# Window attention and expert routing on one Trainium2 core: last logits in column groups, weight loads behind the gather, 128-token products first

## The chip, the cores and the metric

The kernel runs on one core of one Trainium2 chip, alone. The metric is the time of one execution on the device in microseconds (us); the median of several runs counts. The engines are TensorE (PE; its weight loads are listed apart as PEld), VectorE (DVE), ScalarE (ACT), GpSimd (POOL) and SyncE (SP). Each works through its own queue in order. Direct transfers are issued by SP and travel on the hardware queue; indirect ones (gather, scatter) and accumulating ones are issued by POOL and travel on the software queue. Both share 16 DMA engines.

## What is computed

Eight batches of 8 heads attend over 576 positions of 64 numbers, four heads in a window of 32 and four in a dilated one (every fourth of 128). The result x (4608 tokens of 512 numbers) goes through a router that gives each of 8 experts exactly 576 tokens, greedily by the largest logit, and then through that expert's two layers.

```python
attn = softmax(mask(q @ k.T / 8)) @ v
x = attn.transpose(0, 2, 1, 3).reshape(4608, 512)
logits = x @ w_gate
for idx in np.argsort(-logits.flatten()):
    tok, e = idx // 8, idx % 8
    if assigned[tok] < 0 and counts[e] < 576:
        assigned[tok] = e; counts[e] += 1
for e in range(8):
    mask = assigned == e
    out[mask] = np.maximum(x[mask] @ w1[e], 0) @ w2[e]
```

## The kernel before

Three stages follow one another. In **attention** each batch has units (kind of window, part), and each unit makes scores (L503, L506), exponentials on ACT (L456), products with v (L514, into px), a reciprocal and scaling on DVE (L520, L526, into xs) and transposes of xs on TensorE (L564), which ACT or DVE copies to xt (L272, L575). Both forms are needed: xs goes to DRAM as `xd`, and xt is what the logits are made from. Most batches make logits with the gate weights `wgp` (32 columns, 8 of them used) as the stationary operand and 288 tokens moving, the four groups g of 128 features side by side in four column groups of TensorE (L597), copied by DVE (L605) and transposed (L618). The last batch, b=7, goes through `tokens()` (L650) instead: xt is stationary there, 128 tokens at a time, 8 columns of wgp move (L664), and four operations, one for each g, have five products each: four with 128 tokens and one with 64. The results go to `Lt` (L674 and an ACT copy at L272). `R.choose` then takes each token's largest logit (M, L879), and `coarse` counts (L770).

The **router** searches the threshold at which the first expert is full, on DVE and TensorE in turn, then makes its token list `idx` (L1068 to L1102).

The **experts** take eight rounds. In a round r, SP reads the expert's number (`fetch`), POOL gathers its 576 tokens from xd in five indirect transfers (`gather`, L1249: chunks of 128, the last of 64), TensorE transposes each chunk (L1263), and ACT and DVE split it into a high and a low part, `xh` and `xl` (L1137, L1138). From round 1 on these transposes share one buffer, `ptx`. `weights(n, r, f)` loads 256 KB of w1 or w2 into a `raw` buffer (L1150), and ACT makes the high part; the low part is a DVE subtraction or, for w2 of round 0 and for w1 and w2 of round 1, an ACT copy of −high and an accumulating transfer on POOL's queue (L1158, L1160). `expert` makes GEMM1 in pieces `first(f, j)`: f is one of 8 groups of 128 hidden features, j one of two parts of the tokens, 256 or 320 wide, and a piece has 12 products (L1300: high·high, low·high, high·low for four groups of input features). GEMM2 (L1342 to L1347) adds up y, and POOL scatters it (L1368). The search for the next round (counts at L778 with ACT's copy `ohr` of the flags, a step on DVE at L815 to L828) stands among the products of the round before, and so do the gather and the transposes of every round but the first.

The order on each engine is made by a planner, `Schedule`, from operations with an engine, a cost, dependencies and a boost; what it writes out is then that engine's queue. `keep_clock` (L121) puts dummy products on TensorE where the planner sees a gap ahead of the transposes of round 0. `behind(r, f)` gives the planner a dependency of the loads of round 0 from f=3 on upon the gather's second transfer; it shapes the order, and SP's queue holds no wait for it. Round 0 has eight w1 and four w2 loads that find free buffers.

```python
RAW1, D_R, NQ, AHEAD_W = 8, 262, (2, 2), (3,)
MSZ = (128, 128, 128, 128, 64)
CUT = (0, 256, CAP)
```

Of the kernel before, what the change touches and what calls it, by code (L numbers as in the profile page):

```python
# [22 lines left out]
NE, FF = 8, 1024  # L23
# [16 lines left out]
RAW1, D_R, NQ, AHEAD_W = 8, 262, (2, 2), (3,)  # L40
# [202 lines left out]
def attention(tc, ctx, C, load_const, T, xd, Lt, R):  # L243
# [406 lines left out]
    def tokens(un):  # L650

        b, u = un.b, un.u
        c0, c1 = b * S // 128, (b * S + S) // 128
        parts = [(c, 0, 128) for c in range(-(-b * S // 128), c1)]
        half = (c0, 64, 64) if b % 2 else (c1, 0, 64)
        late = B_K if b < B - 1 else B_E
        pt = Buf(PV)
        o = lambda c, p, n: pt.tile[p:p + n, NE * (c - c0):NE * (c - c0) + NE]
# [9 lines left out]
        t = un.op("PE", 1050, lambda: logits([1]), [t], late)  # L668
        t = un.op("PE", 1050, lambda: logits([2]), [t, *ch_[b]], late)
        t = un.op("PE", 1050, lambda: logits([3]), [t, *xt_[b]], late)  # L670
        for kk in range(2):
            xt_[b, kk][2].append(t)
        ca = parts[0][0]
        xs_ = [un.op("DVE", 200, lambda: nc.vector.tensor_copy(  # L674
            Lt[:, ca:c1], pt.tile[:, NE * (ca - c0):NE * (c1 - c0)].rearrange("p (c e) -> p c e", e=NE)), [t], late),
            un.op("ACT", 250, lambda: act(Lt[half[1]:half[1] + 64, half[0]], o(*half)), [t], late)]
        pt.users += xs_
        if b < B - 1:
            hl_.append(xs_[1])
        x = un.op("DVE", 1000, lambda: R.choose(c0, c1), [*xs_, *(hl_ if b == B - 1 else ())], late)  # L680
        coarse(c0, c1, x, B_P if b < B - 1 else late - u * P_U)
# [425 lines left out]
def moe(tc, ctx, C, R, xd, w1, w2, out):  # L1107
# [31 lines left out]
    E, gemm1_end, x_users, got = {}, {}, {}, {}  # L1139

    def weights(n, r, f, deps):

        raw, old, use = RAW[n].take()

# [97 lines left out]
    def gather(r, ix, box):  # L1242

        done = []
        for m, n in enumerate(MSZ):
# [6 lines left out]
            g = op("POOL", 1040, get, [ix, *old], B_G, lat=T_G if r else 2600)  # L1252
# [26 lines left out]
    def gemm(cost, fn, deps):  # L1279
        last[0] = op("PE", cost, fn, [*deps, last[0]])  # L1280
        return last[0]

    def expert(r, X, box, W1, W2):
# [3 lines left out]
        def first(f, j):  # L1287
            ph, old, use = PHR[j].take()
            h, l, hi, lo, useh, usel = W1[f]
            c0, c1 = CUT[j:j + 2]  # L1290
            o = ph[:, :c1 - c0]
            xs = X[:2] if j == 0 else X[2:]
# [11 lines left out]
            for k in range(0, 3 * ND, n):  # L1304
# [7 lines left out]
                g = gemm(n * ((c1 - c0) / 2.4 + 13.5), lambda part=part: mm(part), deps)  # L1312
            useh.append(g)
# [14 lines left out]

        for f, j in ((0, 0), (1, 0), (0, 1), (1, 1), *((f, j) for f in range(2, NF) for j in range(2))):
            first(f, j)  # L1330
# [52 lines left out]
    def round_(r):  # L1383
# [6 lines left out]
        W[r] = [weights("1", r, f, [en, *behind(r, f)]) for f in range(NF)]  # L1390

    def behind(r, f):

        return [got[r, 1]] if r < len(AHEAD_W) and f >= AHEAD_W[r] else []

    round_(0)
    for r in range(NE):
        W2 = [weights("2", r, f, [EN[r], *behind(r, NF)]) for f in range(NF)]
        expert(r, X[r], BOX[r], W[r], W2)
        if r + 1 < NE:  # L1400
            round_(r + 1)
# [78 lines left out]
```

## Time and profile before

| what | value |
|---|---|
| runs | 713.92, 715.23, 717.02 us (median 715.23) |
| the profiled execution's own time | 717.54 us |
| its span, first to last instruction | 715.8 us |
| mean granted TensorE clock | 0.962 of full speed |
| TensorE busy | 673.1 us, 94% of the span |
| VectorE, ScalarE, GpSimd busy | 485.2, 292.0, 137.7 us |
| chain that ended last | TensorE 73%, issue 12%, VectorE 6%, DMA 4%, GpSimd 3% |

The span covers the instructions of the profiled execution; about 1.7 us of its time lie around it. Busy shares are means over stages with different limits, so the rows further down are of single places.

### The profile page before, as it was taken

The numbers are of one execution on the slowest core, as the hardware profiler recorded it, in microseconds if no ns is written. First come the engines' busy times: TensorE is split into PE (matmuls) and PEld (weight loads), VectorE is DVE, ScalarE is ACT, GpSimd is POOL, SyncE is SP. The second block draws the span as 40 slices with busy tenths as digits, with TensorE's granted clock in tenths as the row PEclk, the third lists the DMA queues.
The fourth block names the chain that finished last, engine by engine and source line by source line (L and its number), as shares of the span: only waits on it lengthen the run. The fifth ranks groups of instructions, "written<-read, shape, count | busy, mean of one in ns | idle before, by whom it ended". The sixth has DMA issues, their size and how long they took to land.

```text
span 715.8 us, 17384 instructions
## 1 busy us (share of the span) xinstructions
PE 673.1 (94%) x6577; PEld 590.1 (82%) x6579; DVE 485.2 (68%) x2085; ACT 292.0 (41%) x616; POOL 137.7 (19%) x204
## 2 busy tenths in 40 slices
PE   7899999999974799799999999999999999999995
PEld 5788899989973598689889779879978978988984
DVE  5467867778447789589679878968877964823300
ACT  3345554553520483576234423523523534424310
POOL 6111111100000332641410310310311131221011
PEclk9899999999975799999999999999999999999998
DMA  9999999982210674987323513602621384123001
GB/s 251 267 252 263 277 321 234 281 225 56 68 35 33 212 155 112 286 184 222 97 67 119 170 63 91 217 31 56 227 87 53 124 286 143 50 70 97 1 22 44
DMA packets 58524, 104.60 MB, mean 146 GB/s; under 512 B 6212, under 2 KB 27844, under 8 KB 58436
## 3 DMA queue, kind: packets, MB, share of 16 engines
q1 hardware_dynamic: 49096, 78.32, 38.5%
q0 software_dynamic: 9344, 25.17, 12.8%
q8 instruction: 51, 0.84, 0.5%
q14 instruction: 33, 0.27, 0.1%
HBM read 78.31 MB, written 18.87 MB: 136 GB/s over the span
## 4 chain that ended last, share of the span: by engine, by line
PE 73%; issue 12%; DVE 6%; DMA 4%; POOL 3%; ACT 1%; SPq 0%; POOLq 0%; DVEq 0%
PE ph L1300 24%; PE py L1342 15%; PE pS L506 9%; PE px L514 6%; PE pS L503 3%; PE px L564 3%; DMA xg<-xd,idx 2%; PE pm L486 2%; PE pz L778 2%; PE ptx L1263 2%; PE py L1345 1%; POOL out L1368 1%; PE py L1347 1%; DMA qs<-in_qd 1%; PE px L597 1%
## 5 line engine op out<-in xcount | busy, mean ns | idle before, releaser
L1342 PE MATMUL py<-w2h,hb 128*128 128x512 f32 x512 | 172.5, 401 | 1.3 <-issue 1.3
L1300 PE MATMUL ph<-xh,w1h 128*128 128x256 f32 (+1 forms) x512 | 138.7, 301 | 0.0
L1300 PE MATMUL ph<-xl,w1h 128*128 128x256 f32 (+1 forms) x512 | 136.2, 296 | 0.0
L1300 PE MATMUL ph<-xh,w1l 128*128 128x256 f32 (+1 forms) x512 | 136.0, 296 | 0.0
L1342 PEld LDWEIGHTS py<-w2h,hb 128*128 128x128 f32 x512 | 96.7, 189 | 21.5 <-issue 2.4
L1137 ACT ACTIVATE hb<-ph 128x256 fp32r<-128x256 f32 (+2 forms) x192 | 59.8, 346 | 103.9 <-PE ph L1300 103.5
L1342 PE MATMUL py<-w2l,hb 128*128 128x512 f32 x256 | 100.9, 394 | 0.7 <-DVE w2l L1138 0.5
L1300 PEld LDWEIGHTS ph<-xh,w1h 128*128 128x128 f32 x512 | 91.5, 189 | 0.6 <-ACT xh L1137 0.2
L1300 PEld LDWEIGHTS ph<-xh,w1l 128*128 128x128 f32 x512 | 91.6, 190 | 0.0
L1300 PEld LDWEIGHTS ph<-xl,w1h 128*128 128x128 f32 x512 | 91.5, 190 | 0.0
L506 PE MATMUL pS<-q,k 128*80 128x96 f32 (+1 forms) x672 | 83.7, 266 | 0.0
L1368 POOL DMA_INDIRECT out<-y,idx x40 | 40.1, 1003 | 203.6 <-ACT y L1137 142.8
L1320 DVE SCALAR_TENSOR_TENSOR hb<-ph,hb 128x320 fp32r<-128x320 f32 (+1 forms) x128 | 57.4, 453 | 29.7 <-ACT hb L1137 26.8
L456 ACT ACTIVATE E<-pS 96x384 f32<-96x384 f32 (+1 forms) x96 | 46.8, 487 | 74.9 <-PE pS L506 73.3
L506 PEld LDWEIGHTS pS<-q,k 128*80 128x80 f32 (+1 forms) x672 | 69.2, 160 | 0.3 <-issue 0.3
L1137 ACT ACTIVATE y<-py 128x512 f32<-128x512 f32 (+1 forms) x40 | 23.9, 597 | 103.4 <-PE py L1342 90.8
L493 DVE CUSTOM_DVE_ANT_0 junkm<-pm,const 128x80 bf16<-128x80 f32 (+1 forms) x336 | 59.7, 243 | 7.8 <-PE pm L486 7.5
L1342 PEld LDWEIGHTS py<-w2l,hb 128*128 128x128 f32 x256 | 48.5, 190 | 10.3 <-DVE w2l L1138 1.1
L514 PE MATMUL px<-v,E 81*64 81x65 f32 (+1 forms) x1344 | 48.3, 225 | 4.4 <-ACT E L456 2.5
L514 PEld LDWEIGHTS px<-v,E 81*64 81x64 f32 (+1 forms) x1344 | 43.1, 138 | 9.2 <-issue 2.9
L1137 ACT ACTIVATE w1h<-raw 128x512 fp32r<-128x512 f32 x64 | 38.5, 628 | 29.2 <-DMA raw<-in_moe_w 28.8
L1249 POOL DMA_INDIRECT xg<-xd,idx x40 | 40.3, 1007 | 50.1 <-PE ph L1300 31.1
(171 smaller groups left out, 1019.1 us busy)
## 6 DMA issues: line engine op xcount, KB each, us to landing
raw<-in_moe_w SPq DMA_DIRECT2D x128, 256.0 KB, 4.4
v<-in_vp SPq DMA_DIRECT2D x8, 780.0 KB
v<-in_vd SPq DMA_DIRECT2D x8, 650.0 KB
xd<-xs SPq DMA_DIRECT2D x16, 288.0 KB, 6.8
xd<-xs SPq DMA_DIRECT2D x32, 144.0 KB, 10.6
w2l<-raw POOLq DMA_DIRECT2D x16, 256.0 KB
qs<-in_qp SPq DMA_DIRECT2D x7, 576.0 KB, 9.2
k<-in_kp SPq DMA_DIRECT2D x7, 576.0 KB, 10.4
```

The source lines that it names most:

```text
L456: e = self.op("ACT", 380, lambda j=j, pS=pS: nc.scalar.activation(self.E[:self.nk, j * self.gs:j * self.gs + self.gs], pS.tile[:, :self.gs ...
L493: nc.vector.tensor_tensor_reduce(out=jk[:, c - c0, :nk], in0=pm[:, (c - c0) * nk:(c - c0 + 1) * nk], in1=mm[:, min(1, (c if self.kind == 0 ...
L503: nc.tensor.matmul(pS[:nk, c - c0], ls[:64 + n, c], self.r[:64 + n, :2 * nq], start=(c == c0), stop=False, skip_group_check=True)
L506: nc.tensor.matmul(pS[:nk, c - c0], self.Ks[c], self.Qm[c], start=False, stop=True, skip_group_check=True)
L514: nc.tensor.matmul(px[64 * a:64 * a + 64, c - c0], lh, self.V[c][a], start=True, stop=True)
L564: nc.tensor.transpose(t[:, c], src, C["identf"])
L1137: act = lambda o, i, f=AF.Copy: nc.scalar.activation(o, i, f)
L1249: nc.gpsimd.indirect_dma_start(out=xg[:n], out_offset=None, in_=xd, in_offset=bass.IndirectOffsetOnAxis(ap=box[0][:n, m:m + 1], axis=0))
L1300: nc.tensor.matmul(o, a[:, d * 128:d * 128 + 128], b[:, d, c0:c1], start=((d, i) == pairs[0]), stop=((d, i) == pairs[-1]))
L1320: hl = op("DVE", 335 if j == 0 else 400, lambda: nc.vector.scalar_tensor_tensor(hb[:, CAP + c0:CAP + c1], o, 0.0, hb[:, c0:c1], op0=OP.max ...
L1342: nc.tensor.matmul(py, x, w, start=(f + i == 0), stop=(f == NF - 1 and i == 2))
L1368: s = nc.gpsimd.indirect_dma_start(out=out, out_offset=bass.IndirectOffsetOnAxis(ap=box[0][:n, m:m + 1], axis=0), in_=y[:n], in_offset=None)
```

## The change

Three edits go together.

First, `tokens()`: wgp[:, g] is now stationary and the tokens move; the four chunks of 128 tokens stand side by side in four column groups, and the piece of 64 goes to the first. DVE then copies 128x192 to the tile `lg`, TensorE transposes it back (`gates`), and the two copies to Lt follow. The planner's cost of each of the four groups goes from 1050 to 330.

Second, the weight loads: in round 0 from f=3 on and in round 1 from f=4 on, a POOL memset of one element of the raw buffer, put behind the gather, stands between; the SP load of that buffer waits for it, and all loads behind it on SP's queue with it.

Third, in round 0 the pieces (f=0, j=0) and (f=1, j=0) are each made in two halves of 128 tokens, chunk 0 of both and then chunk 1 of both: 48 products of 128 columns where 24 of 256 stood.

```diff
-RAW1, D_R, NQ, AHEAD_W = 8, 262, (2, 2), (3,)
+RAW1, D_R, NQ, AHEAD_W = 8, 262, (2, 2), (3, 4)
...
-        def logits(gs):
-            for c, p, n in parts + [half]:
-                for g in gs:
-                    t0 = 128 * c + p - b * S
-                    nc.tensor.matmul(o(c, p, n), xt_[b, g // 2][0][:, g % 2, t0:t0 + n], wgp[:, g, :NE],
-                                     start=(c == parts[0][0] and g == 0), stop=(g == 3), skip_group_check=True)
-
-        t = un.op("PE", 1050, lambda: logits([0]), [*xt_[b][:3], ready["w"]], late, pt)
...
+        def logits(g):
+            x = xt_[b, g // 2][0][:, g % 2]
+            for k in range(c1 - c0):
+                nc.tensor.matmul(pt.tile[32 * k:32 * k + 32, :128], wgp[:, g], x[:, t0 + 128 * k:t0 + 128 * k + 128],
+                                 start=(g == 0), stop=(g == 3), skip_group_check=True)
+            nc.tensor.matmul(pt.tile[:32, 128:128 + t0], wgp[:, g], x[:, :t0], start=False, stop=(g == 3), skip_group_check=True)
+
+        t = un.op("PE", 330, lambda: logits(0), [*xt_[b][:3], ready["w"]], late, pt)
...
+        k = un.op("DVE", 330, lambda: nc.vector.tensor_copy(lg[:, :128 + t0], pt.tile[:, :128 + t0]), [t, *L4_["free"]], late)
+        pt.users.append(k)
+
+        def gates():
+            nc.tensor.transpose(pg.tile[:, :128], lg[:, :128], C["identf"])
+            nc.tensor.matmul(pg.tile[128 - t0:, 128:160], lg[:32, 128:128 + t0], C["identf"][:32, :32], start=True, stop=True)
...
         raw, old, use = RAW[n].take()
+        if n == "1" and r < len(AHEAD_W) and f == AHEAD_W[r]:
+
+            gate[r] = op("POOL", 100, lambda: nc.gpsimd.memset(raw[:1, :1], 0.0), [got[r, 1], *old], B_G)
+        if r in gate:
+            deps = [*deps, gate[r]]
...
-            g = op("POOL", 1040, get, [ix, *old], B_G, lat=T_G if r else 2600)
+            g = op("POOL", 1250, get, [ix, *old], B_G, lat=T_G if r else 2500)
...
+        if r == 0:
+
+            two = [PHR[0].take() for _ in range(2)]
+            for m in range(2):
+                ends = [products(f, 0, two[f], X[m:m + 1], 128 * m, 128 * m + 128) for f in range(2)]
+            for f in range(2):
+                hide(f, 0, two[f], ends[f])
         for f, j in ((0, 0), (1, 0), (0, 1), (1, 1), *((f, j) for f in range(2, NF) for j in range(2))):
-            first(f, j)
+            if r or f > 1 or j:
+                first(f, j)
...
-    def behind(r, f):
-
-        return [got[r, 1]] if r < len(AHEAD_W) and f >= AHEAD_W[r] else []
```

`products` and `hide` are `first` cut in two: its twelve products, and what ACT and DVE do with their sum.

How the order on the engines moves is seen at three places. The first is TensorE at the end of attention; L514 are the last products with v, L564 transposes, L664 (after: L662 and L664) the logits of b=7. Before:

```order
L506 MATMUL pS_137<-q_102,k_98 80x96 x4
L664 MATMUL px_139<-wgp,xt_126 128x8 x4
L664 MATMUL px_139<-wgp,xt_126 64x8
L514 MATMUL px_140<-v_104,E_111 64x65 x3
L514 MATMUL px_140<-v_104,E_111 64x65 [waits Activation_49]
L514 MATMUL px_140<-v_104,E_111 64x65 x8
L564 MATMUL px_138<-const_63,xs_122 128x128 [waits DVE_49]
L564 MATMUL px_138<-const_63,xs_122 128x128 x2
L564 MATMUL px_140<-const_63,xs_122 128x128 [waits DVE_49]
L564 MATMUL px_140<-const_63,xs_122 128x128 x2
L664 MATMUL px_139<-wgp,xt_126 128x8 [waits DVE_49,Activation_49]
L664 MATMUL px_139<-wgp,xt_126 128x8 x3
```

After:

```order
L514 MATMUL px_140<-v_104,E_111 64x65 x8
L564 MATMUL px_139<-const_63,xs_122 128x128 [waits DVE_49]
...
L564 MATMUL px_139<-const_63,xs_122 128x128 [waits Activation_49]
L564 MATMUL px_139<-const_63,xs_122 128x128 x2
L662 MATMUL px_138<-xt_124,wgp 32x128 [waits Activation_49]
L662 MATMUL px_138<-xt_124,wgp 32x128 x3
L664 MATMUL px_138<-xt_124,wgp 32x64
...
L662 MATMUL px_138<-xt_126,wgp 32x128 [waits DVE_49,Activation_49]
L662 MATMUL px_138<-xt_126,wgp 32x128 x3
L664 MATMUL px_138<-xt_126,wgp 32x64
L676 MATMUL px_140<-const_63,L_127 128x128 [waits DVE_49]
L677 MATMUL px_140<-const_63,L_127 64x32
```

Before, three of the four logits groups stand ahead of the last L514 (two of them above these rows); after, all four stand behind the last transposes, four sets of which now follow L514, and behind them the two products of `gates`.

The second place is TensorE at the start of round 0, where xg is the gathered chunk, `ph` the sum of GEMM1 and L778 (after: L782) a count of the search. Before:

```order
L1263 MATMUL py_3205<-const_63,xg_3252 128x128 [waits DMASW0_49]
L1263 MATMUL py_3205<-const_63,xg_3252 128x128 x3
L121 LDWEIGHTS zero
L121 MATMUL ph_3202<-zero 128x512
L1263 MATMUL py_3206<-const_63,xg_3253 128x128 [waits DMASW1_49]
...
L1263 MATMUL ptx_3207<-const_63,xg_3254 128x128 [waits DMASW2_49,DVE_49]
L1263 MATMUL ptx_3207<-const_63,xg_3254 128x128 x3
L1300 MATMUL ph_3201<-xh,w1h_3220 128x256 [waits Activation_49]
L1300 MATMUL ph_3201<-xh,w1h_3220 128x256 x3
L1300 MATMUL ph_3201<-xh,w1l_3236 128x256 x4
L1263 MATMUL py_3205<-const_63,xg_3255 128x128 [waits DMASW3_49,DVE_49]
```

After:

```order
L1272 MATMUL py_3208<-const_63,xg_3255 128x128 [waits DMASW0_49]
L1272 MATMUL py_3208<-const_63,xg_3255 128x128 x3
L782 LDWEIGHTS ohr [waits Activation_49]
L782 MATMUL pz<-G,ohr 128x4x16 [waits DVE_49]
...
L1272 MATMUL py_3209<-const_63,xg_3256 128x128 [waits DMASW1_49]
L1272 MATMUL py_3209<-const_63,xg_3256 128x128 x3
L1308 MATMUL ph_3204<-xh,w1h_3223 128x128 [waits Activation_49]
L1308 MATMUL ph_3204<-xh,w1h_3223 128x128 x3
L1308 MATMUL ph_3204<-xh,w1l_3239 128x128 x4
L1272 MATMUL ptx_3210<-const_63,xg_3257 128x128 [waits DMASW2_49]
L1272 MATMUL ptx_3210<-const_63,xg_3257 128x128 x3
L1308 MATMUL ph_3204<-xl,w1h_3223 128x128 [waits DVE_49]
```

GEMM1 (L1300, after: L1308) began behind the transposes of three chunks and now begins behind those of two; the nine counts, which stood behind 40 products of GEMM1, now stand between the two chunks' transposes, and the single dummy products between them are gone.

The third place is POOL, SP and ACT in round 1. POOL before (w1l is an accumulating transfer, out a scatter, xg the gather):

```order
L1160 DMA w1l_3236<-raw_3208 128x512 [waits DMASW6_49,DMAHW0_49,PE_49,Activation_49]
L1160 DMA w1l_3237<-raw_3209 128x512 [waits DMASW7_49,DMAHW1_49,PE_49,Activation_49]
L1160 DMA w1l_3238<-raw_3210 128x512 [waits DMASW0_49,DMAHW2_49,PE_49,Activation_49]
L1367 MEMSET spacer 1x1 [waits Pool_49]
L1368 DMA out<-y_3269,idx 4608x512 [waits DMASW1_49,Activation_49]
L1249 DMA xg_3252<-xd,idx 128x512 [waits DMASW2_49,DVE_49]
L1249 DMA xg_3253<-xd,idx 128x512 [waits DMASW3_49]
...
L1249 DMA xg_3256<-xd,idx 64x512 [waits DMASW6_49]
L1160 DMA w1l_3239<-raw_3211 128x512 [waits DMASW7_49,DMAHW3_49,PE_49,Activation_49]
L1160 DMA w1l_3240<-raw_3212 128x512 [waits DMASW0_49,DMAHW4_49,PE_49,Activation_49]
```

POOL after:

```order
L1394 MEMSET spacer 1x1 [waits Pool_49]
L1395 DMA out<-y_3272,idx 4608x512 [waits DMASW1_49,Activation_49]
L1258 DMA xg_3255<-xd,idx 128x512 [waits DMASW2_49,DVE_49]
L1258 DMA xg_3256<-xd,idx 128x512 [waits DMASW3_49]
...
L1258 DMA xg_3259<-xd,idx 64x512 [waits DMASW6_49]
L1150 MEMSET raw_3215 1x1
L1169 DMA w1l_3242<-raw_3214 128x512 [waits DMASW7_49,DMAHW3_49,PE_49,Activation_49]
L1394 MEMSET spacer 1x1 [waits Pool_49]
L1395 DMA out<-y_3273,idx 4608x512 [waits DMASW0_49,Activation_49]
L1169 DMA w1l_3243<-raw_3215 128x512 [waits DMASW1_49,PE_49,DMAHW4_49,Activation_49,Pool_49]
```

SP after, in the same round (raw_3215 is the buffer of f=4):

```order
L1159 DMA raw_3213<-in_moe_w 128x512 [waits DMAHW2_49,DVE_49]
L1159 ISA
L1159 DMA raw_3214<-in_moe_w 128x512 [waits DMAHW3_49,DVE_49]
L1159 ISA
L1159 DMA raw_3215<-in_moe_w 128x512 [waits DMAHW4_49,DVE_49,Pool_49]
L1159 ISA
L1159 DMA raw_3216<-in_moe_w 128x512 [waits DMAHW5_49,DVE_49,Activation_49]
L1159 ISA
L1159 DMA raw_3219<-in_moe_w 128x512 [waits DMAHW6_49,DMASW1_49,Activation_49]
```

ACT after, in the same round:

```order
L1141 ACTIVATE xh<-ptx_3210 128x4x128 [waits PE_49]
L1141 ACTIVATE xh<-ptx_3210 128x4x128 [waits DVE_49,PE_49]
L1141 ACTIVATE w1h_3227<-raw_3215 128x512 [waits DMAHW4_49,Pool_49]
L1141 ACTIVATE y_3271<-py_3209 128x512 [waits DMASW5_49,PE_49]
L1167 ACTIVATE w1l_3243<-w1h_3227 128x512 [waits Activation_49]
L1141 ACTIVATE w1h_3228<-raw_3216 128x512 [waits DMAHW5_49]
L1141 ACTIVATE xh<-ptx_3210 128x4x128 [waits DVE_49,PE_49]
```

POOL's memset follows the fifth gather, the load of f=4 waits for it on SP, and eight more loads stand behind that one. On ACT the split of f=4 (w1h_3227) now stands behind xh of chunks 0 and 1 and ahead of a y, and that of f=5 ahead of xh of chunk 2.

## Rows read from the trace of the kernel before

**Rows 1.** The page, part 2: TensorE in 40 slices of 17.9 us.

```profile
PE   7899999999974799799999999999999999999995
```

**Rows 2.** Chain that ended last, 195 to 212 us: start us, us, what.

```profile
195.55 1.11 PE px L597 x16
198.54 0.33 PE px L564 x3
198.87 1.00 PE px L664 x10
204.92 0.76 PE px L514 x23
206.61 0.56 PE px L564 x3
207.20 0.67 DVE xt L575
208.01 2.17 PE px L664 x10
210.63 0.21 DVE M L879
```

**Rows 3.** Windows: length, busy us (instructions) by engine, granted clock, DMA share, GB/s.

```profile
208.00:210.00 2.00, 1.99 (x10) 1.98 (x10) 0.00 (x0) 0.00 (x0) 0.00 (x0) 0.50 0.65 166
```

**Rows 4.** Timeline, round 0: start, us, engine, line, what, [idle before].

```profile
237.33 1.45 POOL L1249 DMA_INDIRECT xg<-xd,idx  x1 [3.35 <-DVE idx L1102]
240.50 0.46 DVE L889 TENSOR_TENSOR oh<-Lt,Mo 128x288 bf16<-128x288 f32 x1
242.97 0.66 PE L1263 MATMUL py<-const,xg 128*128 128x128 f32 x4 [1.75 <-DMA xg<-xd,idx]
244.97 0.74 PE L1300 MATMUL ph<-xh,w1h 128*128 128x256 f32 x4
245.53 1.16 ACT L902 ACTIVATE ohr<-oh 128x1152 bf16<-128x1152 bf16 x1
248.47 0.64 PE L1300 MATMUL ph<-xl,w1h 128*128 128x256 f32 x4
```

**Rows 5.** Windows, columns as in rows 3: round 0's gather, then round 2's.

```profile
230.00:241.50 11.50, 6.17 (x31) 2.37 (x30) 10.84 (x30) 2.27 (x4) 4.58 (x4) 0.51 0.90 307
341.75:342.25 0.50, 0.50 (x4) 0.42 (x3) 0.50 (x2) 0.50 (x1) 0.32 (x1) 1.00 0.00 0
342.25:343.50 1.25, 1.25 (x8) 1.02 (x7) 1.25 (x4) 0.04 (x1) 0.97 (x1) 1.00 0.77 210
```

**Rows 6.** Timeline of POOL: first gather of round 2.

```profile
340.54 1.08 POOL L1249 DMA_INDIRECT xg<-xd,idx  x1 [7.13 <-issue]
```

**Rows 7.** Timeline, round 1: weight loads on SP, gathers, ACT, TensorE.

```profile
279.55 32.42 SPq L1150 DMA_DIRECT2D raw<-in_moe_w  x13
289.25 1.04 POOL L1249 DMA_INDIRECT xg<-xd,idx  x1 [0.30 <-DVE A L1049]
294.38 0.92 POOL L1249 DMA_INDIRECT xg<-xd,idx  x1 [0.30 <-issue]
298.55 0.63 ACT L1137 ACTIVATE w1h<-raw 128x512 fp32r<-128x512 f32 x1 [4.68 <-DMA raw<-in_moe_w]
298.76 0.66 PE L1263 MATMUL ptx<-const,xg 128*128 128x128 f32 x4 [4.00 <-DMA xg<-xd,idx]
```

**Rows 8.** Windows, columns as in rows 3: before and behind the wait in round 1.

```profile
289.50:294.50 5.00, 5.00 (x31) 3.90 (x29) 3.20 (x11) 3.76 (x6) 3.78 (x5) 1.00 1.10 263
299.10:302.70 3.60, 3.60 (x20) 2.91 (x19) 2.17 (x9) 1.19 (x3) 3.00 (x6) 0.54 1.11 207
```

**Rows 9.** DMA, 289 to 291 us: software queue's packets, MB, share of 16 engines.

```profile
q0 software_dynamic: 133, 0.25, 67.5%
```

**Rows 10.** Timeline of weight loads of GEMM1, round 0.

```profile
255.01 0.19 PEld L1300 LDWEIGHTS ph<-xh,w1h 128*128 128x128 f32 x1
255.12 0.19 PEld L1300 LDWEIGHTS ph<-xh,w1l 128*128 128x128 f32 x1
```

More of the change, by code (lines that the diff above doesn't have):

```diff
@@ L652, in tokens @@
         b, u = un.b, un.u
[L653 to L655 removed]
+        c0, c1 = -(-b * S // 128), (b * S + S) // 128
+        t0 = 128 * c0 - b * S
         late = B_K if b < B - 1 else B_E
[L657 to L665 removed]
@@ L667, in tokens @@
[L667 to L670 removed]
+        pt, pg = Buf(PV), Buf(PV)
+        lg = L4.tiles[0][:, (b % 2) * S:]
+        def logits(g):
[4 more added lines that the diff above has]
+            nc.tensor.matmul(pt.tile[:32, 128:128 + t0], wgp[:, g], x[:, :t0], start=False, stop=(g == 3), skip_group_check=True)
@@ L671, in tokens @@
+        t = un.op("PE", 330, lambda: logits(0), [*xt_[b][:3], ready["w"]], late, pt)
+        t = un.op("PE", 330, lambda: logits(1), [t], late)
+        t = un.op("PE", 330, lambda: logits(2), [t, *ch_[b]], late)
+        t = un.op("PE", 330, lambda: logits(3), [t, *xt_[b]], late)
         for kk in range(2):
             xt_[b, kk][2].append(t)
-        ca = parts[0][0]
-        xs_ = [un.op("DVE", 200, lambda: nc.vector.tensor_copy(
-            Lt[:, ca:c1], pt.tile[:, NE * (ca - c0):NE * (c1 - c0)].rearrange("p (c e) -> p c e", e=NE)), [t], late),
-            un.op("ACT", 250, lambda: act(Lt[half[1]:half[1] + 64, half[0]], o(*half)), [t], late)]
@@ L683, in attention @@
+        t = un.op("PE", 180, gates, [k], late, pg)
+        xs_ = [un.op("DVE", 200, lambda: nc.vector.tensor_copy(
+            Lt[:, c0:c1], pg.tile[:, :128].rearrange("p (c e) -> p c e", e=32)[:, :, :NE]), [t], late),
+            un.op("ACT", 250, lambda: act(Lt[128 - t0:, c0 - 1], pg.tile[128 - t0:, 128:128 + NE]), [t], late)]
+        pg.users += xs_
+        x = un.op("DVE", 1000, lambda: R.choose(c0 - 1, c1), [*xs_, *hl_], late)
+        coarse(c0 - 1, c1, x, late - u * P_U)
     ch_, hl_ = {}, []
@@ L1285, in expert, with products @@
         hidden = {}
[L1287 to L1292, printed above, removed]
+        def products(f, j, ring, xs, c0, c1):
+            ph, old, _ = ring
+            h, l, hi, lo, _, _ = W1[f]
+            o = ph[:, c0 - CUT[j]:c1 - CUT[j]]
             pairs = [(d, i) for d in range(ND) for i in range(3)]
@@ L1327, in first @@
                 done.append(h2)
+        def first(f, j):
+            ring = PHR[j].take()
+            hide(f, j, ring, products(f, j, ring, X[:2] if j == 0 else X[2:], *CUT[j:j + 2]))
+        if r == 0:
[4 more added lines that the diff above has]
+                hide(f, 0, two[f], ends[f])
         for f, j in ((0, 0), (1, 0), (0, 1), (1, 1), *((f, j) for f in range(2, NF) for j in range(2))):
-            first(f, j)
+            if r or f > 1 or j:
+                first(f, j)
         gemm1_end[r] = last[0]
@@ L1389, in round_ @@
         X[r] = gather(r, ix, BOX[r])
-        W[r] = [weights("1", r, f, [en, *behind(r, f)]) for f in range(NF)]
-    def behind(r, f):
-        return [got[r, 1]] if r < len(AHEAD_W) and f >= AHEAD_W[r] else []
+        W[r] = [weights("1", r, f, [en]) for f in range(NF)]
     round_(0)
     for r in range(NE):
-        W2 = [weights("2", r, f, [EN[r], *behind(r, NF)]) for f in range(NF)]
+        W2 = [weights("2", r, f, [EN[r]]) for f in range(NF)]
         expert(r, X[r], BOX[r], W[r], W2)
```

13 lines of the change are left out of this document (7 added, 6 removed).

## The prediction

> **What bounds the kernel now.** I read the page's slices first. TensorE's row stands at nine nearly everywhere and falls in two places: slices 11 to 13 (197 to 250 us: the end of attention, the router's search, the start of round 0) and slice 16 (286 to 304 us: the start of round 1) [rows 1]. All three edits act there, so each place is read by itself; elsewhere the time is TensorE's own work, and a part that moves no TensorE work there changes nothing.
>
> End of attention, by the chain of work that ended last [rows 2]: up to 205.68 it is TensorE all the way, and three of its pieces are logits groups of L664 (the first is shown, 1.00; three alike make 3.0). After the last score-times-value products (204.92 + 0.76) no TensorE work covers anything: scale, transposes, the DVE copy of xt, then the fourth logits group, 2.17 long, and the router's first instruction M at 210.63. The window shows why that group took twice as long as the other three: granted clock 0.50, the lower of the two levels, 1.2 GHz [rows 3], behind the 0.83 between the transposes' end (207.17) and 208.01 in which TensorE only waited for the copy.
>
> Start of round 0, by the timeline [rows 4]: the first gather is issued at 237.33; TensorE, busy with dummy products until 241.22, then waits 1.75 for the chunk and starts transposing at 242.97. GEMM1 starts at 244.97 and its part j=0 of f=0,1 ends at about 248.95 (the last four start at 248.47). The windows show the DMA engines at a 0.90 share, 307 GB/s, up to 241.5, when twelve weight loads are under way [rows 5]. For comparison round 2's gather, issued at 340.54 on idle queues, has no data until 342.25 and carries it in the next 1.25 us [rows 5, 6]: about 3.0 us from issue to landed chunk.
>
> Start of round 1 [rows 7]: weight loads are issued from 279.55 on, the first gather at 289.25, the last of its five at 294.38, but TensorE waits 4.00 us for the first chunk, until 298.76. In 289.5 to 294.5 the DMA share is 1.10 [rows 8]; the software queue, which carries the gather and ahead of it three accumulating w1l transfers and a scatter, moves only 0.25 MB in 289 to 291, one chunk's worth [rows 9]. After the stall the granted clock is 0.54 for 3.6 us [rows 8]: of these about 1.7 are lost (3.6 × 0.46). So this place costs 5.7.
>
> **Part 1, logits (A).** Before, the three covered groups cost 3.0 on the path, and two transposes of another unit stood ahead too (0.33 each [rows 2]); by the order both now stand behind the last products. So those end at about 205.68 − 3.0 − 0.66 = 202.0. From there: normalizing as before (0.93: 205.68 to 206.61), transposes 0.56, a copy of xt 0.67, making 204.2. Then twenty logits products: L597, which puts 288 columns in the same column groups, runs 16 in 1.11 [rows 2]; the new ones have at most 128 columns. They cannot be cheaper than that by much (0.069 each), so five of the last group 0.35, up to 1.4 for all twenty if nothing is ready earlier. The added copy of 128x192 is bounded by the Lt-sized DVE instruction (M, 0.21) and the xt copy (0.67): I take 0.35. The added transposes are two of a trio that takes 0.33 to 0.56: 0.3. The copies to Lt as before: 0.45 from the end of the group at 210.18 to M. Six hand-overs at 0.03 to 0.04 give 0.2. The sum is 205.8 to 206.9 at the full clock; at half clock transposes and logits double, up to 207.6. M was at 210.63: a gain of 3.0 to 4.8. I take **A = −3.4**, on the cold side, since TensorE stands there as before. If side-by-side groups ran one after another (20 at the 0.10 that L664 pays) and cold, the gain would fall to about 1.5.
>
> **Part 2, round 0 (B).** The loads of f=3 on wait behind the POOL memset, which stands behind all five gathers, so only three of twelve compete with the gather. Chunk 0 lands at 237.33 + 3.0 to 3.3, 240.6 at the latest, before the dummies end: the wait of 1.75 goes. But the order puts the first nine counts (0.46) between the transposes of chunks 0 and 1. They need ACT's copy ohr: its source is ready at 240.96 and it takes 1.16 [rows 4], thus 242.15. Then: transposes 241.22 to 241.88, counts to 242.65, chunk 1's transposes to 243.3, GEMM1 from there (244.97 before), a gain of 1.7. Against it stand 48 products of 128 columns in place of 24 of 256. The trace has none with such weights. Those of 256 columns follow one another at about 0.12 (24, with 1.06 of transposes among them, in 244.97 to 248.95). The lower bound from columns alone would be half of that, 0.06; the upper is 0.12, no change per product. The nearest row is the weight load: at a change of operand two of 128 columns start 0.11 apart [rows 10], and the L664 products, eight columns wide with the same 128-column weights, take 0.10 each [rows 2]. That is weight load and nothing else, so I take 0.115: 48 × 0.115 = 5.5 against 24 × 0.12 = 2.9. With the transposes of chunks 2 to 4 between (0.6, 0.6, 0.46) part j=0 ends at 243.3 + 5.5 + 1.7 = 250.5; the counts in it (0.46) stood later before. **B = 250.5 − 0.46 − 248.95 = +1.1**; by 0.06 a product it would be −1.5.
>
> The rule that bears on this: the Trainium skill, "TensorE: Matmul & The Clock Gate", section "Back-to-back issue gap", gives about 81 ns for each pair of weight load and 128-column product in a stream. By it the sum would be 1.6 lower (48 × 0.034); no row here shows so short a pair with fp32r weights of 128 columns, so it is a rival below.
>
> The gated loads cost nothing here: f=3's issue at about 244 plus 3 to 4 us is 248, while f=0 to 2 cover it: 36 products of 256 columns at 0.12 and 36 of 320 at, by their columns, 0.15 are 9.7 from 243.3 on, so f=3 is due at 253 or later. With that cover gone, each us is a us.
>
> **Part 3, round 1 (C).** Ungated are only f=0 to 3, issued from 279.55: 1.05 MB, which at the 307 GB/s of [rows 5] is through by 283, well ahead of the gather; f=4 and the eight loads behind it on SP's queue stay away until about 295.6. The software queue then has its three transfers and scatter done near 290, and chunk 0, at 3.0 us from issue, lands at 292.3 to 293. TensorE comes to it at 294.76. Stall and clock drop go: −5.7. Late next is DVE: the order puts a search step ahead of xl, and the single transpose buffer then holds the next chunk up; I give 0.4 for it. **C = −5.3**, between −6 and −3.
>
> What the gate delays: behind the load of f=4 on ACT stand y of m=3 and, behind f=5, xh of chunk 2 (order above). f=4 lands at about 295.6 + 3 = 298.6, f=5 near 299.5; xh of chunk 2 ran at 306.07 before, so is due at about 300.5. A us or so of slack. GEMM1 of round 1 takes f=4 about 13 us after its start, far behind. In before ACT itself stood for f=7's load until 298.55, ahead of all xh [rows 7]; that wait now comes behind chunks 0 and 1.
>
> **The rest (D)**: in rounds 3 to 7 counts and ranks stand about one group earlier. TensorE is at nine tenths or more in each of those slices, with nothing long to win: 0, give or take 1.
>
> **Sum**: −3.4 + 1.1 − 5.3 = −7.6, from the profiled execution's own 717.54 to 709.9. That execution lies 2.3 above the median 715.23, so against the runs shown: **707.6**.
>
> **Rivals.**
> *128-column products are cheap* (0.06 to 0.08 each): B turns −0.5 to −1.5, total 705.0 to 706.0. For it: no row has a stream of them, and the 0.11 is one change of operand; against: [rows 10], and L664 beside it.
> *Column groups serial, or tail cold throughout*: A = −1.5, total 709.5. Against it is L597.
> *The round-1 gather stays late*: the accumulating transfers and the scatter on its own queue, not the loads, hold it. For it: the software queue alone reaches a share of 67.5% in 289 to 291 [rows 9]. Then 2 to 4 us of stall and part of the low clock remain, C = −1 to −3, total 710 to 712.
> *The gate itself becomes the wait* (the slower side): ACT is in order, so a gated load f=4 or f=5 that lands late holds xh of chunk 2, the single transpose buffer and TensorE. If the nine loads meet a gather still in its queue (1.2 MB at 0.13 MB/us, the rate of [rows 9], is 9 us: 304), the stall is 4 plus a low clock of 1.7, so C is near 0, total 713. It makes the kernel slower by 0.5% only if f=5 lands more than 11 us behind its due time, after about 311.5; then 719 and up.
> *Reordered later rounds open new waits*: several of 1 to 2 us, total 709 to 711.
>
> **Chances.** Main case 0.47 (705.5 to 709.5); cheap products 0.14; tail 0.09; gather late 0.14; gate 0.10, of which 0.03 slower; later rounds 0.06. The bound of 0.5% (about what a measurement of this kernel can tell from no change) is 711.65 and 718.8. Faster: all of main, cheap, tail, 0.05 of later rounds and 0.09 of gather late: 0.84; slower 0.03; the same 0.13. For 8 in 10 the range is 703.0 to 712.5: it leaves out the gate case and the best ends of all parts together.
>
> **What would show it.** Right: M some 3 to 4.5 us earlier; no wait for xg before the first transposes of either round; the granted clock at 1.0 behind round 1's gather; 128-column products spaced 0.11 or more. Wrong: spacing of 0.08 or less (B); a TensorE wait on xg near 293 (C); ACT waiting for raw with xh behind it; SP's gated loads landing after 301.

## The result, and the profile after

The changed kernel ran at 706.46, 708.50, 709.66 and 710.48 us, median 709.08, against 716.01 for four runs of the kernel before: ratio 0.9876, 95% interval 0.9827 to 0.9925. The forecast was 707.6, a change of −7.6; the measured one is −6.9. A second set of runs gave 0.9847 (0.9803 to 0.9890). So the sum held. Its terms did not: they erred on both sides and cancelled, which is luck.

The profiled execution took 706.46 us, the fastest of the four, while that of before (717.54) was slower than all four of its own, so the two spans lie 11.2 apart, more than the medians. The page after, to be read beside [rows 1]:

```profile
span 704.6 us, 17434 instructions
...
PE   7899999999964999899999999999999999999995
...
PEclk9999999999985899999999999999999999999998
```

Counted from 0, slice 13, the start of round 0, now stands at nine; slices 11 and 12 still hold the search, and slice 16 is at eight where it was at seven. Next the chain of the changed kernel at the end of attention (start us, us, what), which answers to [rows 2]:

```profile
195.60 0.87 PE px L514 x24
...
198.04 0.92 PE px L564 x6
198.96 0.40 PE px L662 x8
...
199.40 0.28 PE px L662 x6
...
200.55 0.37 DVE L L672
...
200.97 0.33 PE px L676
...
202.06 0.21 DVE M L883
```

The chain leaves the products with v at 196.47 for DVE (the last of them end at 197.15 in the timeline), not at 205.68, and M starts at 202.06, not at 210.63. The logits now are one run of 0.40, 0.28 and so on behind the transposes, about 1.5 in all, where the last group alone took 2.17, but DVE's copy and the transposes back follow: from the last products to the first gather both kernels take the same time, 31.6 and 31.7.

Behind M the stages run like this (TensorE, its weight loads and POOL in the timeline: start, us, engine, line, what, idle before and what ended it), beside [rows 4]:

```profile
228.75 1.46 POOL L1258 DMA_INDIRECT xg<-xd,idx  x1 [3.35 <-DVE idx L1106]
...
232.66 0.44 PEld L1272 LDWEIGHTS py<-const,xg 128*128 128x128 f32 x4 [0.93 <-DMA xg<-xd,idx]
232.66 0.68 PE L1272 MATMUL py<-const,xg 128*128 128x128 f32 x4
...
233.64 0.46 PE L782 MATMUL pz<-G,ohr 128*128 128x64 bf16 x9 [0.29 <-issue]
...
234.48 0.64 PE L1308 MATMUL ph<-xh,w1h 128*128 128x128 f32 x4
...
240.10 0.61 PE L1308 MATMUL ph<-xh,w1h 128*128 128x128 f32 x4
...
240.55 0.61 PE L1308 MATMUL ph<-xh,w1l 128*128 128x128 f32 x4
...
241.00 0.61 PE L1308 MATMUL ph<-xl,w1h 128*128 128x128 f32 x4
...
241.44 0.80 PE L1308 MATMUL ph<-xh,w1h 128*128 128x320 f32 x4
```

The transposes start 3.9 behind the gather's issue, where it was 5.6. TensorE shows no wait for the chunk, but only because its dummy products end at 232.64, just when the chunk is there; the first weight load had waited 0.93 for it. Fours of 128-column products start at 240.10, 240.55, 241.00 and 241.44, so one product takes 0.112. And round 1, beside [rows 7]:

```profile
281.67 1.03 POOL L1258 DMA_INDIRECT xg<-xd,idx  x1 [0.30 <-DVE A L1053]
...
286.98 0.46 PE L782 MATMUL pz<-G,ohr 128*128 128x64 bf16 x9
...
287.28 0.63 PE L1272 MATMUL ptx<-const,xg 128*128 128x128 f32 x4
...
290.47 0.32 DVE L819 STREAM_TRANSPOSE Q<-pz 128x128 f32<-128x128 f32 x1 [3.67 <-remote]
290.53 0.60 ACT L1141 ACTIVATE xh<-ptx 128x512 fp32r<-128x512 f32 x1 [4.79 <-remote]
...
292.62 0.45 PE L782 MATMUL pz<-G,ohr 128*128 128x64 bf16 x9 [2.63 <-DVE G L796]
```

The transposes of chunk 0 start at 287.28 with no wait, 5.6 after the gather's issue. But the 4.00 of before is not simply gone. The nine counts ahead of them end at 287.44, and DVE, which only needs their result (Q), starts at 290.47; ACT starts xh at 290.53, though its transposes ended at 287.91. "Remote" means that the profile found the update of the semaphore that both waited for, just ahead of their start, and no instruction that ended there. TensorE, which has recorded products up to 289.99, then stands until DVE's step is done, at 292.62, and the low clock follows (windows: length, busy us by engine, granted clock, DMA share, GB/s; compare [rows 8]):

```profile
281.70:287.20 5.50, 5.50 (x39) 4.26 (x38) 3.29 (x12) 1.76 (x2) 4.28 (x5) 1.00 0.73 214
290.00:292.60 2.60, 0.00 (x0) 0.00 (x0) 1.96 (x9) 0.60 (x1) 0.09 (x1) 1.00 0.93 232
294.20:297.60 3.40, 3.40 (x10) 2.47 (x9) 1.89 (x6) 2.00 (x4) 0.00 (x0) 0.50 0.92 351
```

So the gather meets a DMA share of 0.73 where it met 1.10, and still TensorE lost 2.6 and then half of the 3.4 that it ran at a granted clock of 0.50, which is 1.2 GHz.

From starts in the traces of all profiled executions one gets a table by stage. "v" is the end of the last products with v, "gather" the first gather's issue in round 0, G1 and G2 the first product of GEMM1 and GEMM2 in a round, "the end" the start of the last instruction. Rows in bold are the kernel before and the changed one.

| kernel | start to v | v to gather | gather to G2, round 0 | to G1, round 1 | to G1, round 2 | to the end |
|---|---|---|---|---|---|---|
| **before** | 205.66 | 31.67 | 37.02 | 36.01 | 58.43 | 346.93 |
| **before, again** | 205.22 | 31.67 | 37.12 | 35.92 | 58.45 | 345.41 |
| **changed** | 197.15 | 31.60 | 37.99 | 35.91 | 59.24 | 342.63 |
| **changed, again** | 198.20 | 31.59 | 37.90 | 32.78 | 59.40 | 343.05 |
| tokens_only | 197.16 | 31.60 | 39.97 | 37.02 | 58.44 | 344.83 |
| tokens_undone | 206.34 | 31.67 | 37.87 | 31.21 | 60.48 | 343.30 |
| no_gate | 201.72 | 31.61 | 40.17 | 35.49 | 58.93 | 342.70 |
| gate1_only | 201.49 | 31.61 | 40.14 | 31.23 | 60.50 | 342.67 |
| split_undone | 203.31 | 31.61 | 36.62 | 31.20 | 58.94 | 343.26 |
| cost_back | 196.46 | 31.60 | 38.68 | 30.54 | 60.11 | 343.11 |
| tokens_1050 | 202.98 | 31.34 | 37.86 | 31.23 | 60.53 | 342.62 |
| no_split_cost | 198.41 | 31.62 | 37.24 | 30.65 | 60.62 | 342.92 |

The kernels below the bold rows are the experiments that follow. Ratios are to runs of the kernel before on the same chip; the two kernels again, no_gate and tokens_only ran on one chip (chip 2), tokens_1050 and no_split_cost on another (3) and the other four on a third (13). Which chip the first profiles of the two kernels are from is not on record.

### The profile page after: what moved, and what is told of

It reads as the page before. It is cut to its first block, busy times and chain, and to the rows that moved or that the text cites. A ratio compares the mean times of both kernels' runs of the same rounds, so it can differ in the third digit from the quotient of the medians.

```text
span 704.6 us, 17434 instructions
## 1 busy us (share of the span) xinstructions
PE 667.7 (95%) x6602; PEld 586.8 (83%) x6604; DVE 484.9 (69%) x2086; ACT 291.8 (41%) x616; POOL 137.9 (20%) x206
## 4 chain that ended last, share of the span: by engine, by line
PE 68%; issue 12%; DVE 9%; DMA 6%; POOL 2%; ACT 1%; another core or an unknown queue 1%; POOLq 0%; SPq 0%; DVEq 0%
PE ph L1308 18%; PE py L1369 18%; PE pS L506 8%; PE px L514 5%; DMA qs<-in_qd 3%; PE px L564 3%; PE pS L503 2%; PE pm L486 2%; PE ptx L1272 2%; PE pz L782 2%; PE py L1372 1%; PE py L1374 1%; DMA v<-in_vd 1%; DVE hb L1335 1%; POOL out L1395 1%
## 5 line engine op out<-in xcount | busy, mean ns | idle before, releaser
L1308 PE MATMUL ph<-xh,w1h 128*128 128x256 f32 (+2 forms) x520 | 139.2, 299 | 0.0
L1308 PE MATMUL ph<-xl,w1h 128*128 128x256 f32 (+2 forms) x520 | 138.0, 297 | 0.0
L1308 PE MATMUL ph<-xh,w1l 128*128 128x256 f32 (+2 forms) x520 | 137.0, 295 | 0.0
L1308 PEld LDWEIGHTS ph<-xh,w1h 128*128 128x128 f32 x520 | 92.8, 190 | 0.5
L1308 PEld LDWEIGHTS ph<-xh,w1l 128*128 128x128 f32 x520 | 92.7, 190 | 0.0
L1308 PEld LDWEIGHTS ph<-xl,w1h 128*128 128x128 f32 x520 | 92.4, 190 | 0.1
L514 PE MATMUL px<-v,E 81*64 81x65 f32 (+1 forms) x1344 | 47.0, 224 | 1.8 <-ACT E L456 1.7
L514 PEld LDWEIGHTS px<-v,E 81*64 81x64 f32 (+1 forms) x1344 | 42.1, 137 | 6.4 <-ACT E L456 1.8
```

The lines of the kernel that those rows point to most:

```text
L514: nc.tensor.matmul(px[64 * a:64 * a + 64, c - c0], lh, self.V[c][a], start=True, stop=True)
L1308: nc.tensor.matmul(o, a[:, d * 128:d * 128 + 128], b[:, d, c0:c1], start=((d, i) == pairs[0]), stop=((d, i) == pairs[-1]))
```

## The experiments

**The two kernels once more** (no edit).

> The changed kernel a second time, nothing altered. In its first profile the end of attention lies 8.5 us earlier than before where the steps gave 3.7, the first products of round 1 gain nothing over the gather of round 0 where the steps gave 5.3 (TensorE idle 2.63 at 290.0 behind a hold of its semaphore, then the low clock 3.4 us), and rounds 2 to 6 gain 4.3. Theory 1 (chance of one execution): the hold in round 1 and the early part of attention are not the kernel's; a second profile has no TensorE idle over 1 us in round 1, GEMM1 of round 1 about 4 us sooner behind the gather, and the end of attention at about 200 instead of 197.1. Theory 2 (the order): both come back within 1 us. Time 707 to 711 by either.

> The kernel before a second time, nothing altered. Theory 1 (chance): TensorE's waits and low clock between 15 and 60 us differ from the first profile, with the end of attention 2 to 5 us earlier than 205.7; the waits of round 1 (4.0) and of rounds 3 to 6 (3.2 in all) come back, for they stand in the order. Theory 2: attention ends at 205 to 206.5 again. Time 714 to 717; ratio 0.998 to 1.002, which is the noise of all that follows.

The changed kernel: 706.48 us median, 0.9847 (0.9803 to 0.9890). The kernel before against its own runs: 0.9971 (0.9925 to 1.0016), so half a per cent is indeed what one set of runs cannot tell. The end of attention came at 198.20 and 205.22: it stays with the kernel, so theory 2 holds there (no_gate and gate1_only, with the same attention, end it at 201.72 and 201.49, so some of it is chance all the same).

In round 0 the transposes again start 3.9 behind the gather's issue (229.79), but here the dummy products had ended earlier and TensorE waited:

```profile
233.67 0.66 PE L1272 MATMUL py<-const,xg 128*128 128x128 f32 x4 [1.26 <-DMA xg<-xd,idx]
```

In round 1 neither theory held whole. The late semaphore came back, smaller (timeline, changed kernel again):

```profile
287.92 0.46 PE L782 MATMUL pz<-G,ohr 128*128 128x64 bf16 x9
...
289.94 0.32 DVE L819 STREAM_TRANSPOSE Q<-pz 128x128 f32<-128x128 f32 x1 [2.40 <-PE ptx L1272]
...
292.09 0.45 PE L782 MATMUL pz<-G,ohr 128*128 128x64 bf16 x9 [1.16 <-DVE G L796]
```

The counts end at 288.38 and DVE starts at 289.94; TensorE stands 1.16 instead of 2.63, and no low clock follows. In rounds 3 to 6 the kernel before lost less than in its first profile (waits of TensorE, 340 to 700 us: engine line, waited for, us, times, longest; the first profile, then this one):

```profile
PE py L1342 <- issue: 1.5, 3, 0.7
PE pz L778 <- DVE G L792: 1.2, 1, 1.2
PE py L1342 <- DVE w2l L1138: 0.5, 2, 0.2
```

```profile
PE py L1342 <- issue: 0.9, 2, 0.7
PE pz L778 <- DVE G L792: 0.5, 1, 0.5
PE py L1342 <- DVE w2l L1138: 0.5, 2, 0.2
```

In all 1.9 where the first profile had 3.2, with the same instructions in the same order: part of these waits is chance.

**no_gate**: the memsets write elsewhere, every instruction keeps its place.

```diff
+    free = pw.tile([1, 1], F32, name="free")
...
-            gate[r] = op("POOL", 100, lambda: nc.gpsimd.memset(raw[:1, :1], 0.0), [got[r, 1], *old], B_G)
+            gate[r] = op("POOL", 100, lambda: nc.gpsimd.memset(free, 0.0), [got[r, 1], *old], B_G)
```

> The changed kernel with every instruction in its place, but the two memsets write a tile of their own, so no load waits. If the gate is worth what the prediction says, the first chunk is late again in both rounds: a wait of 1 to 2 us in round 0 and of 2 to 5 us, with the low clock behind it, in round 1; 5 to 7 us slower than the changed kernel, 713 to 716. If the wait in round 1 only moved (the rival), the time is within 2 us of the changed kernel, 707 to 711.

713.04 us, 0.9934 (0.9895 to 0.9973), and 6.6 more than the changed kernel on the same chip. The waits are back (waits of TensorE, 230 to 300 us):

```profile
PE ptx L1273 <- DMA xg<-xd,idx: 3.1, 1, 3.1
PE py L1273 <- DMA xg<-xd,idx: 2.2, 1, 2.2
```

Round 0 takes 40.17 instead of 37.9, round 1's stretch 35.49 where the changed kernel on the same chip took 32.78. Of the difference between these two profiles 3.5 lies in attention, which the edit does not touch, so the 6.6 is not the gate's alone; that the wait merely moves is refuted.

**gate1_only**: as no_gate, with the memset of round 1 alone on raw.

```diff
-            gate[r] = op("POOL", 100, lambda: nc.gpsimd.memset(raw[:1, :1], 0.0), [got[r, 1], *old], B_G)
+            gate[r] = op("POOL", 100, lambda: nc.gpsimd.memset(raw[:1, :1] if r == 1 else free, 0.0), [got[r, 1], *old], B_G)
```

> The changed kernel with every instruction in its place, but the memset of round 0 writes a tile of its own, so only round 1's loads wait. Round 0 then shows the wait of the kernel without gates (2.19, with low clock behind it; from the gather's issue to GEMM2 40.2 instead of 37.9), round 1 the stretch of the changed kernel (32.8 to 35.9): 2 us slower than the changed kernel. If the gate of round 0 is worth nothing, within 0.5 us of it.

709.63 us, 0.9908 (0.9874 to 0.9941). Round 0 took 40.14, round 1's stretch 31.23, with no late semaphore though every instruction stands where it stands in the changed kernel. The gate of round 0 is worth 2.2, as expected. What the gate of round 1 does to the gather shows most plainly between these two runs (no_gate: timeline; gate1_only: DMA issues, with the us from issue to landing):

```profile
288.61 1.03 POOL L1259 DMA_INDIRECT xg<-xd,idx  x1 [0.30 <-DVE Mo L1061]
...
297.28 1.11 PE L1273 MATMUL ptx<-const,xg 128*128 128x128 f32 x4 [3.07 <-DMA xg<-xd,idx]
```

```profile
xg<-xd,idx POOLq DMA_INDIRECT x1, 3.5
```

Without the gate the first chunk is there 8.7 behind its issue, with it 3.5. The stretch is 4.3 shorter than in no_gate, which had a late semaphore itself (1.7) and ran on another chip, so part of the 4.3 may be due to these.

**tokens_only** and **tokens_undone**: the function `tokens()` of the change in the kernel before, and that of before in the changed kernel.

> The kernel before with the logits of the last batch in column groups alone; gates, split and planner costs of the experts as before. By the prediction A = -3.4: 711 to 713. By the first profile of the changed kernel, were all of its 8.5 the order's: 706 to 708. TensorE's idle times of rounds 3 to 6 (3.2 in all) should stay, as the experts' order is that of before.

> The changed kernel with the logits of the last batch as before. With the experts' gates, halves and order alone: the last products with v end at 205 to 206 again, and from the gather of round 0 on the times are those of the changed kernel, 3 to 5 us less than before: 710 to 712 at a kernel before of 715.2. If the early end of attention were chance it would show here too (197 to 202).

tokens_only: 711.46 us, 0.9913 (0.9876 to 0.9951), by the ratio some 6 us faster than before. tokens_undone: 710.77 us, 0.9916 (0.9879 to 0.9954). The end of attention followed the function: 197.16 with the new one, 206.34 with the old, so it is not chance. tokens_only won more in attention than the forecast's 3.4 and lost 4.0 of it again in the ungated rounds 0 and 1 (39.97 and 37.02 against 37.0 and 36.0). The waits of rounds 3 to 6 were there, 1.1 in all.

**tokens_1050**: the cost of the four groups back at 1050, so that three of them stand ahead of the last products with v again.

```diff
-        t = un.op("PE", 330, lambda: logits(0), [*xt_[b][:3], ready["w"]], late, pt)
+        t = un.op("PE", 1050, lambda: logits(0), [*xt_[b][:3], ready["w"]], late, pt)
...
```

> The changed kernel with the planner's cost of the four logits groups back at 1050: the products are those of the change, but three of the four groups stand ahead of the last products with v again, as before, and the order of attention is nearly that of before. If the gain at the end of attention comes from the products being cheaper, each group takes 0.3 to 0.4 on the path instead of 1.0 and the stretch from the 187th product with v (about 40 us) to the last one, net of idle time and low clock, is 159 (160.9 in three profiles of the old logits, 156.9 in seven of the new), with the rest won behind the last products, where the last group and what follows is 1.5 to 2.5 us shorter than in the changed kernel's order. If idle time in that stretch (2.0 to 3.7 in the old order, 0.6 to 2.3 in the new) hangs on the order, it is 2 to 3.7 here. In all within 1.5 us of the changed kernel.

708.43 us, 0.9890 (0.9832 to 0.9948). The chain shows the groups at 0.44 each (0.35 + 0.09), as expected:

```profile
197.24 0.35 PE px L662 x8
197.59 0.09 PE px L664 x2
...
199.26 0.36 PE px L662 x8
...
201.54 0.35 PE px L662 x8
...
205.32 0.43 PE px L662 x8
```

But the stretch net of idle time and low clock was 160.0, not 159, and behind the last products only 0.25 was won, not 1.5 or more: the last group ran in 0.51, and what follows it, copy, transposes and copies, fills the time that it gave back. Idle time was 1.58, between the old and the new orders. So, by this one profile, the cheaper products by themselves bring about 1 us; the rest of the 4.0 that the groups behind the last products bring (step A below) comes with where they stand.

**split_undone**: the two first pieces whole.

```diff
-        if r == 0:
-
-            two = [PHR[0].take() for _ in range(2)]
-            for m in range(2):
-                ends = [products(f, 0, two[f], X[m:m + 1], 128 * m, 128 * m + 128) for f in range(2)]
-            for f in range(2):
-                hide(f, 0, two[f], ends[f])
...
-            if r or f > 1 or j:
-                first(f, j)
+            first(f, j)
```

> The changed kernel with the first two pieces of round 0 whole again: 24 products of 256 columns. By the prediction (B = +1.1 net, 2.6 of it the doubled products, 1.7 given back by the earlier start) GEMM1 of round 0 starts some 2 us later and its sum of products is 2.6 us shorter: the kernel is 0.5 to 1.5 us faster than the changed one. By the rival (a 128-column product at half price) it would be 0.5 to 1.5 us slower.

706.55 us, 0.9842 (0.9799 to 0.9884), not to be told from the changed kernel by time. In the trace the stage from the gather to G2 took 36.62 instead of 37.9: 1.3 less, inside the forecast and against the rival.

**cost_back**: the planner's cost of a gather as before.

```diff
-            g = op("POOL", 1250, get, [ix, *old], B_G, lat=T_G if r else 2500)
+            g = op("POOL", 1040, get, [ix, *old], B_G, lat=T_G if r else 2600)
```

> The changed kernel with the planner's cost of a gather back at 1040 and its latency in round 0 at 2600: the counts then stand where they stood before (round 0: behind GEMM1's first pieces; round 1: behind the transposes of chunk 0), while column groups, gates and halves stay. In both profiles of the changed kernel, and in the one without gates, TensorE's semaphore for the count that stands ahead of round 1's first transposes came 1 to 3 us late. If that place is the cause, no such delay shows here, TensorE does not stand over 0.5 us in round 1, and from GEMM2 of round 0 to GEMM1 of round 1 it takes 30 to 32 us (36.0 before, 35.9 and 32.8 in the changed kernel). If the delay is chance, it is not bound to this order and the stretch is 32 to 36. The gain of rounds 2 to 7 (2.2 to 4.3) stays only if it does not hang on the counts' new places. Time 704 to 711 scaled to a kernel before of 715.2.

706.83 us, 0.9863 (0.9825 to 0.9901). In round 1 the transposes now stand ahead of the count, and DVE follows without delay (timeline):

```profile
287.00 0.60 PE L1272 MATMUL ptx<-const,xg 128*128 128x128 f32 x4
...
287.44 0.45 PE L782 MATMUL pz<-G,ohr 128*128 128x64 bf16 x9
287.64 0.60 ACT L1141 ACTIVATE xh<-ptx 128x512 fp32r<-128x512 f32 x1 [1.88 <-PE ptx L1272]
...
288.87 0.30 DVE L819 STREAM_TRANSPOSE Q<-pz 128x128 f32<-128x128 f32 x1
```

The stretch to round 1 is 30.54, as forecast. The gain of rounds 2 to 7 stayed (343.1). From GEMM1 of round 2 on, TensorE, DVE, ACT and POOL here work through the same sequence of instructions, told by their tiles, as in the kernel before, so that gain does not hang on the new order of these rounds.

**no_split_cost**: split_undone and cost_back together.

> Column groups and gates of the change, first pieces of round 0 whole, a gather's planner cost at 1040. From the gather of round 0 to GEMM2 36.6 or a little more (37.9 in the changed kernel, 36.6 with the halves undone), from there to GEMM1 of round 1 30.5 (32.8 to 35.9 in the changed kernel, 30.5 with the cost back): 1.3 + 0.7 us less than the changed kernel without its late semaphore. 702 to 707 scaled to a kernel before of 715.2. If the halves pay for themselves in this order, no gain over the one with the cost back.

704.80 us, 0.9849 (0.9800 to 0.9899). Round 1's stretch came out at 30.65, round 0 at 37.24, and the rounds from 2 on, again in the sequence of the kernel before, at 342.92. In round 0, in this order and without the halves, TensorE stands ahead of the transposes of four of the five chunks, 2.6 in all. Its median is the lowest measured here, but its interval and those of the changed kernel cover one another, so no version is shown to beat it.

## Why the prediction was right in sum, and where its steps failed

**A, the logits: right in kind, too small.** The step said −3.4 and held everything ahead of the tail fixed but 3.66 us of moved work. Eight profiles with the new groups behind the last products end attention at 196.46 to 203.31, mean 199.2; three with the old logits at 205.22 to 206.34, mean 205.7: −6.5. To split this I took the stretch from the 187th product with v (39 to 43 us) to the last and took off TensorE's idle time and half of the time at the low clock: 160.8, 160.8 and 161.1 in the old, 156.7 to 157.6 in the eight new ones. So the work moved off the path is 4.0, near the 3.66. The rest: TensorE's idle time in that stretch, which the step held constant, is 2.1 to 3.7 in the old profiles (mean 3.0) and 0.2 to 2.3 in the new ones (mean 1.2), 1.9 less; about 0.7 lies ahead of the stretch, where two profiles of the changed kernel differ by as much. That the new order lessens the idle time is not shown: the ranges overlap. The tail was sized right: copy, transposes and copies take what the last group gives back. Its bound for a cold tail was summed too low (206.9 with transposes and logits doubled is about 209, not 207.6), but the tail ran at a granted clock of 1.00.

**B, round 0: right in size, one step by luck.** +1.1 was forecast; gather to G2 takes 37.9 to 38.0 instead of 37.0 to 37.1, +0.9. A 128-column product costs 0.112 against the 0.115 assumed; that is near the pace of the weight loads in [rows 10], 0.11, though that the load sets it is argued, not shown. Undoing the halves saves 1.3. The step that failed is the chunk's landing. It was put at 3.0 to 3.3 behind the issue, with the transposes starting 3.9 behind it because of the dummy products. They do start there, but on the chunk: with the gate of round 0 it lands 3.8 to 3.9 behind the issue in every profile that tells, and TensorE's wait of 1.75 became one of 0 to 1.5, by where the dummies end. The rival built on cheap products falls. The rule of the Trainium skill ("TensorE: Matmul & The Clock Gate", section "Back-to-back issue gap") would have made a product about 0.081; with these fp32r weights the 0.112 measured decides.

**C, round 1: the mechanism right, the outcome in the changed kernel not.** −5.3 was forecast. The gated gather lands in time, as the step said (gate1_only, above). Where TensorE's semaphore is not late, the stretch from G2 of round 0 to G1 of round 1 is 31.2 in four kernels with the changed order and 30.5 to 30.7 with the counts behind the transposes: −4.8 and −5.4. In the two profiles of the changed kernel it was 0 and −3.2, and in the first the granted clock behind the gather was 0.50, not the 1.0 that was to show the step right. The step that failed is "late next is DVE ... I give 0.4": TensorE stood 2.6 and 1.2 for DVE, and not for DVE's own work but for an update that came late to it. ACT standing behind the gated loads, the rival on the slow side, did not happen: ACT's wait ahead of xh is the same late update.

**D, the rest: the step that failed outright.** It said 0 ± 1, from slices at nine tenths with "nothing long to win". From G1 of round 2 to the end three profiles, the kernel before twice and tokens_only, take 344.8 to 346.9, and the other nine 342.6 to 343.3: −2.8 between the means. About half of it is idle time of TensorE (3.2, 1.9 and 1.1 in the three, 0.2 to 0.9 in the nine), in waits each too short to show in a slice; the other half lies in the products and is not explained.

The new order of these rounds is not needed for it: cost_back and no_split_cost have the sequence of the kernel before there and take 343.1 and 342.9. What these two have in common with the other seven, and the three longer ones lack, is the gates in the planner's input, with `behind` gone; that loads really wait is not needed either, as no_gate keeps the gain. But these two were profiled on chips 13 and 3, where the kernel before was not, so how much of the −2.8 belongs to the gates, the order, the chip and chance stays open.

Against the gain stands a wait that all nine have (waits of TensorE, 302 to 340 us, in the changed kernel and then in gate1_only):

```profile
PE pz L1028 <- DVE ge L991: 1.1, 1, 1.1
```

```profile
PE pz L1028 <- DVE ge L991: 2.4, 1, 2.4
```

In these nine GEMM1 of round 1 to that of round 2 takes 0.5 to 2.2 more than the 58.4 of the three. So of −6.5, +0.9, −1.6 (the mean of the two profiles), +0.9 and −2.8 (these means, with a before of 345.7 for the last) the sum is −9.1, between the two measured changes (−6.9 and, by 0.9847, −11.0). A forecast of −7.6 hit it because A and D were taken too small and C too large.

What stays open besides D: why TensorE's semaphore is late. In round 1 it was late in three of the profiles in which a count stands right ahead of the first transposes (the changed kernel twice, no_gate) and not late in four others with the same order, so that order alone does not bring it. Nor is it needed, for the first profile of the kernel before shows a late update in a later round, with no count ahead of the transposes (they end at 459.70, ACT starts at 460.64):

```profile
459.10 0.60 PE L1263 MATMUL ptx<-const,xg 128*128 128x128 f32 x4
...
460.64 0.60 ACT L1137 ACTIVATE xh<-ptx 128x512 fp32r<-128x512 f32 x1 [0.82 <-PE ptx L1263]
```

What divides the profiles as well is where they were taken: the six from chips 13 and 3 hold no late update that DVE or ACT stood for, and all that hold one are from chip 2 or the first set. The six profiles of chip 2 and the first set also hold fewer updates of TensorE's semaphore than instructions that make one (696 for 704 in the changed kernel), and the other six do not. So the chip or its recording is a rival that no run here separates from the order.

## What to carry to other kernels

A load that competes with a gather on the critical path can be held back by a real wait on its queue; that pays only as far as TensorE would have waited, so size it from the wait and from what stands behind the loads: here the first chunk of round 1 landed 3.5 behind its issue instead of 8.7. When a planner makes the order, changing a cost moves work everywhere: compare stage by stage over several profiles, since one pair of profiles mixes the edit with chance, and take both kernels on each chip. Before a gain is put down to a new order, see whether a kernel in the old order has it too. Halving the width of products need not halve their cost: here one of 128 columns cost 0.112 where one of 256 cost 0.12, so the halves cost more than the earlier start gave back (by 1.3 in split_undone, by 1.4 between cost_back and no_split_cost).

## What was not expected of the hardware

An update of TensorE's semaphore came 1 to 3 us after the end recorded for the instruction that makes it (290.45 for 287.44 in the changed kernel), while TensorE's next products were recorded without a gap up to 289.99. The update of the transposes, which end 0.47 later, came only 0.06 behind it. And the first 40 us differ from run to run: the place of the 187th product with v lay between 39.2 and 42.6 us in profiles whose instructions up to there differ little, with the granted clock at 0.50 for anything from 0 to 6.8 us of it.
